# Gate and up weights of a gated MLP beside attention: three buffers and two pairs ahead instead of two buffers and one pair ahead

## The chip, the cores and the metric

One core of one Trainium2 chip. The time of a run is device microseconds from start to end of one launch. All runs quoted here are fast: none lies over 1.5% above the fastest run of its kernel. A profile is one traced execution; its span, first to last instruction, is some 1.8 us shorter than the time of the same run (468.2 against 470.01). Each run also lists the mean clock granted to TensorE, 1.0 being full speed.

## The reference

A transformer block over 2048 tokens of width 448, in bf16: a layernorm, then attention (16 heads of 28, full softmax) and a gated MLP (1792 wide) side by side, all summed.

```
xn = layernorm(x)
q, k, v = split(xn @ wqkv)
o = softmax(q @ k.T * scale) @ v
h = gelu(xn @ w_gate) * (xn @ w_up)
return x + o @ wo + h @ w_down
```

## The kernel before

The kernel runs attention and MLP interleaved. ScalarE takes the exponentials of the scores, 442 tiles of 128x1024; VectorE approximates 70 more. TensorE multiplies the scores into three PSUM buffers, from which ScalarE or VectorE takes them, and fills the time between with everything else: projections, value products, gate, up and down matmuls. A small scheduler in the kernel's own source decides at build time in which order each engine's stream stands. At run time the streams are fixed, and semaphores alone hold them back.

The gate and up matmuls work in pairs of 128 columns. A pair's weights are one tile of 224 KB. There are 28 gate pairs and 28 up pairs: four blocks of 512 tokens, seven pairs each, and the weights are read again for each block.

```python
wgupool = ctx.enter_context(tc.tile_pool(name="wgu", bufs=2))
spool = ctx.enter_context(tc.tile_pool(name="spsum", bufs=3, space=bass.MemoryType.PSUM))
...
def load_w(nm, n):
    if n < NQ * NFC // 2 and (nm, n) not in mlp_w:
        pr = n % (NFC // 2)
        mlp_w[(nm, n)] = w = wgupool.tile([DCH, NDC, 2 * P], BF16, tag=nm, name=nm)
        nc.sync.dma_start(w[:], (wg_v if nm == "wg" else wu_v)[:, :, pr * 2 * P : (pr + 1) * 2 * P])
...
def g_up(Q, pr):
    ht = ht_tiles[(Q, pr)]
    n = Q * NPR + pr
    load_w("wu", n + 1)
    w = mlp_w.pop(("wu", n))
    ...
    for k in range(2):
        ps = aux_tile([P, QT], F32, "up")
        for c in range(NDC):
            yield mm(ps[:], w[:, c, k * P : (k + 1) * P], xnc(Q, c), c == 0, c == NDC - 1, T_MM)
        yield ("ev", T_MM, C_EVAC, lambda k=k, ps=ps: f(k, ps), [("ht", Q, pr, k)])
```

(`g_gate` is the same with "wg". Cuts are marked by "...".) All loads stand in SyncE's queue, in order, together with the small copies that spread the softmax reciprocals. Twice in the kernel ScalarE does 14 GELUs in one batch, at 134 and at 352 us. TensorE uses that time for a run of up pairs, back to back.

The softmax here doesn't subtract the row's maximum and nothing guards it: scores larger than these inputs give would overflow.

Of the kernel before, what the change touches and what calls it, by code (L numbers as in the profile page):

```python
# [38 lines left out]
def kernel(  # L39
# [20 lines left out]
    TPQ = QT // P  # L60
    SCALE = float(Dh) ** -0.5
    NU = NQ * NHG * NKC * 4
    NB = 19
    NVA = 6
    NE = 12
    HALF_MM = 112
# [18 lines left out]
    drpool = ctx.enter_context(tc.tile_pool(name="dr", bufs=3, space=bass.MemoryType.DRAM))  # L85
    onpool = ctx.enter_context(tc.tile_pool(name="on", bufs=6))
    respool = ctx.enter_context(tc.tile_pool(name="res", bufs=2))
    wgupool = ctx.enter_context(tc.tile_pool(name="wgu", bufs=2))
    spool = ctx.enter_context(tc.tile_pool(name="spsum", bufs=3, space=bass.MemoryType.PSUM))
    aux = ctx.enter_context(tc.tile_pool(name="aux", bufs=1, space=bass.MemoryType.PSUM))  # L90

# [18 lines left out]
    wv_ap = A_wqkv.rearrange("(c p) f -> p c f", p=DCH)  # L110
    wst0_t = bpool.tile([P, 2, QT], BF16, tag=f"b{NB - 1}", name="wst0")
    wst0 = wst0_t[0:DCH].rearrange("p a b -> p (a b)")[:, 0 : NDC * 8 * Dh].rearrange(
# [45 lines left out]
# [5 lines that stand above are left out]
# [12 lines left out]
    def xnc(T, c):  # L175
        return xnT0[c // 2][:, c % 2, :] if T == 0 else xnT[T][:, c, :]
# [8 lines left out]
    for lo, hi in LNB:  # L185
        n = hi - lo
# [90 lines left out]
    def aux_tile(shape, dt, name):  # L277
        return aux.tile(shape, dt, tag=bank[0], name=name)

    def mm(ps, lhsT, rhs, start, stop, cost):  # L280
        def emit(lo, hi, cols):
            sl = slice(None) if start else slice(lo, hi)
            for m in range(0, P, P // cols):
                nc.tensor.matmul(  # L284
                    ps[m : m + P // cols, sl],
                    lhsT=lhsT[:, m : m + P // cols],
                    rhs=rhs[:, sl],
                    start=start,
                    stop=stop,
                    skip_group_check=True,  # L290
                    **({"tile_position": (0, m)} if cols > 1 else {}),
                )

        return ("mm", cost, emit, 1 if start else rhs.shape[-1])
# [57 lines left out]

    b_free = list(range(NB))
    b_used = {}
    n_otsb = [0]

    def big(kind, key, shape, dt, name):
        n = b_free.pop(0)
        b_used.setdefault((kind, key), []).append(n)
        return bpool.tile(shape, dt, tag=f"b{n}", name=name)  # L360

    def g_gate(Q, pr):
        ht = ht_tiles[(Q, pr)] = big("h", Q, [P, 2, QT], BF16, "ht")
        n = Q * NPR + pr
        load_w("wg", n + 1)
        w = mlp_w.pop(("wg", n))

        def f(k, ps):
            nc.vector.tensor_copy(ht[:, k, :], ps[:])  # L369
            mlp_done[0] += 1  # L370

        for k in range(2):
            ps = aux_tile([P, QT], F32, "gate")
            for c in range(NDC):
                yield mm(ps[:], w[:, c, k * P : (k + 1) * P], xnc(Q, c), c == 0, c == NDC - 1, T_MM)
            yield ("ev", T_MM, C_EVAC, lambda k=k, ps=ps: f(k, ps), [("g", Q, pr, k)])

    def g_up(Q, pr):
        ht = ht_tiles[(Q, pr)]
        n = Q * NPR + pr  # L380
        load_w("wu", n + 1)
        w = mlp_w.pop(("wu", n))

        def f(k, ps):
            nc.vector.tensor_mul(ht[:, k, :], ps[:], ht[:, k, :])  # L385
            mlp_done[0] += 1
# [6 lines that stand above are left out]
# [292 lines left out]
    for n, batch in enumerate(BATCHES):  # L685
        for Q in batch:
            mlp_items(Q, g_gate, GATE_AT, lambda pr: xkeys(Q), room)
        for Q in batch:
            mlp_items(Q, g_up, UP_AT, lambda pr: [("gelu", Q, pr)], None)
            out_items(Q)  # L690
# [36 lines left out]
    nc.scalar.preload_act_table(AF.Sqrt)  # L727
    xf = bpool.tile([P, 2, QT], BF16, tag=f"b{NB - 2}", name="xf")[:].rearrange("p a b -> p (a b)").bitcast(F32)[:, 0:D]
    mv1 = L["mv"][:, 1, :]
# [583 lines left out]
```

## Time and profile before

| | before |
|---|---|
| time, median of the 3 runs before the prediction | 469.35 us (469.03 to 470.36) |
| span of the profiled run | 468.2 us |
| busy: TensorE, ScalarE, VectorE | 95%, 95%, 77% |
| TensorE idle for late weights | 8.4 us (up), 2.2 us (gate) |
| ScalarE idle for scores | 7.8 us, 1.4 of it before the kernel has got going |

In the views below, a timeline line has the start and the length in us, the engine, the source line, the operation with its tiles, the number of instructions merged into it, and in brackets the idle time before it with what ended it. A line of the list of waits has the total in us, the number of waits and the longest. A line of the groups has the busy time and the mean duration in ns, then the idle time before.

### The profile page before, as it was taken

The page shows a single profiled execution, that of the slowest core. Times are in us where ns is not written, and L with a number is a line of the kernel's source. Part 1 is how long each engine was busy: PE and PEld are TensorE (multiplying, and loading weights), DVE is VectorE, ACT ScalarE, POOL GpSimd, SP SyncE. Part 2 cuts the span into 40 slices and gives each one's busy share as a digit, 9 for nine tenths or more (in the row PEclk, how much of TensorE's full clock was granted, in tenths as well). Part 3 has the DMA queues.
Part 4 walks back from the last instruction along what each step waited for, and adds up shares of the span by engine and source line. Part 5 has one row for each costly group of instructions (what it writes and reads, how often), then busy time and mean ns, then how long its engine had stood idle before and what let it go on. Part 6 is the DMA issues. An engine that isn't in the chain of part 4 may idle for free.

```text
span 468.2 us, 11309 instructions
## 1 busy us (share of the span) xinstructions
PE 444.5 (95%) x4659; PEld 163.8 (35%) x4659; DVE 360.6 (77%) x572; ACT 445.2 (95%) x486; POOL 20.0 (4%) x78
## 2 busy tenths in 40 slices
PE   8899999999987999999999999999997899999994
PEld 4333434333233333333333233333333333333431
DVE  5787686889786877899999897879997677855243
ACT  4899999999999899999999999999999899999992
POOL 5512020000000000000000000000000000000000
PEclk9999999999999999999999999999999999999996
DMA  6920112002133101021202101011203200021001
GB/s 172 298 42 1 41 41 59 2 23 61 34 86 90 30 12 24 12 72 41 72 21 72 41 2 34 21 34 53 60 6 88 81 13 23 22 72 41 14 2 40
DMA packets 43220, 22.81 MB, mean 49 GB/s; under 512 B 8480, under 2 KB 43168, under 8 KB 43168
## 3 DMA queue, kind: packets, MB, share of 16 engines
q1 hardware_dynamic: 42272, 21.65, 17.1%
q8 instruction: 36, 0.59, 0.6%
q10 hardware_dynamic: 896, 0.44, 0.3%
q14 instruction: 16, 0.13, 0.1%
HBM read 20.06 MB, written 1.90 MB: 47 GB/s over the span
## 4 chain that ended last, share of the span: by engine, by line
PE 78%; DMA 9%; DVE 6%; ACT 3%; issue 2%; SPq 0%; POOL 0%; ACTq 0%; DVEq 0%; POOLq 0%
PE st L539 22%; PE ot L587 19%; PE op L284 10%; PE gate L284 10%; PE up L284 8%; PE pp L284 5%; DMA wu<-in_B_w_up_dram 4%; ACT e L551 3%; PE pv L284 3%; DMA x<-in_A_x_dram 2%; DVE w L561 2%; DMA wg<-in_B_w_gate_dram 2%; DVE t L579 2%; DVE ht L369 1%; DVE w L579 0%
## 5 line engine op out<-in xcount | busy, mean ns | idle before, releaser
L551 ACT ACTIVATE e<-st 128x1024 bf16<-128x1024 f32 x442 | 406.7, 1191 | 8.1 <-PE st L539 7.8
L539 PE MATMUL st<-qT,kT 28*128 28x512 bf16 x1024 | 134.3, 382 | 2.3 <-ACT e L551 1.5
L561 DVE TENSOR_SCALAR w<-st 128x1024 f16<-128x1024 f32 x70 | 85.4, 1220 | 22.0 <-PE st L539 22.0
L539 PEld LDWEIGHTS <-kT 28*128 28x128 bf16 x1024 | 42.9, 90 | 124.5 <-issue 120.8
L587 PE MATMUL ot<-e,va 128*32 128x512 bf16 x884 | 80.2, 384 | 0.7 <-ACT e L551 0.5
L579 DVE TENSOR_SCALAR t<-w 128x2048 uint16<-128x2048 f16 x105 | 68.7, 680 | 0.3
L284 PE MATMUL up<-xnT,wu 112*32 112x512 bf16 (+2 forms) x631 | 56.8, 380 | 8.9 <-DMA wu<-in_B_w_up_dram 8.4
L284 PE MATMUL gate<-xnT,wg 112*32 112x512 bf16 (+2 forms) x386 | 62.4, 377 | 2.5 <-DMA wg<-in_B_w_gate_dram 2.2
L284 PE MATMUL op<-wd_sb,ht 128*32 128x448 bf16 (+3 forms) x526 | 56.0, 340 | 0.0
L385 DVE TENSOR_TENSOR ht<-up,ht 128x512 bf16<-128x512 f32 x56 | 38.6, 689 | 20.9 <-PE up L284 15.8
L587 PEld LDWEIGHTS <-va 128*32 128x32 bf16 x1444 | 32.9, 95 | 54.8 <-issue 41.4
L369 DVE CAST ht<-gate 128x512 bf16<-128x512 f32 x56 | 38.3, 686 | 5.9 <-PE gate L284 5.6
L587 PE MATMUL ot<-t,va 128*32 128x512 bf16 x420 | 36.4, 382 | 0.9 <-DVE t L579 0.9
L284 PEld LDWEIGHTS <-wu 112*32 112x32 bf16 (+1 forms) x631 | 21.3, 96 | 36.6 <-DMA wu<-in_B_w_up_dram 14.6
L609 DVE TENSOR_TENSOR otsb<-ot,otsb 128x512 f32<-128x512 f32 x36 | 24.7, 687 | 8.2 <-PE ot L587 7.7
L284 PEld LDWEIGHTS <-wg 112*32 112x32 bf16 (+1 forms) x386 | 19.5, 96 | 27.5 <-issue 10.7
L284 PEld LDWEIGHTS <-ht 128*32 128x32 bf16 (+1 forms) x526 | 22.2, 97 | 19.5 <-issue 6.1
L1113 ACT ACTIVATE ht<-ht 128x1024 bf16<-128x1024 bf16 x28 | 26.7, 1041 | 0.0
L579 DVE TENSOR_SCALAR w<-w 128x2048 uint16<-128x2048 f16 x35 | 24.2, 691 | 0.9
L284 PE MATMUL op<-wo_sb,on 128*32 128x448 bf16 (+2 forms) x170 | 17.8, 345 | 0.0
L284 PE MATMUL pp<-xnT,wq_sb 112*32 112x512 bf16 (+2 forms) x105 | 17.8, 369 | 0.0
L284 PE MATMUL pv<-wv,xnT 112*128 112x448 bf16 (+2 forms) x92 | 15.7, 353 | 1.2 <-DVE kT L329 1.2
(95 smaller groups left out, 220.7 us busy)
## 6 DMA issues: line engine op xcount, KB each, us to landing
wg<-in_B_w_gate_dram SPq DMA_DIRECT2D x28, 224.0 KB
wu<-in_B_w_up_dram SPq DMA_DIRECT2D x28, 224.0 KB
bc<-rr SPq DMA_DIRECT2D x60, 32.0 KB
out_dram<-res SPq DMA_DIRECT2D x15, 112.0 KB
wd_sb<-in_B_w_down_dram SPq DMA_DIRECT2D x1, 1568.0 KB
x<-in_A_x_dram SPq DMA_DIRECT2D x3, 448.0 KB
den<-otsb SPq DMA_DIRECT2D x60, 2.0 KB
wst<-in_A_wqkv_dram SPq DMA_DIRECT2D x2, 392.0 KB
```

The costliest lines, as they stand in the source:

```text
L284: nc.tensor.matmul(ps[m : m + P // cols, sl], lhsT=lhsT[:, m : m + P // cols], rhs=rhs[:, sl], start=start, stop=stop, skip_group_check=Tr ...
L369: nc.vector.tensor_copy(ht[:, k, :], ps[:])
L385: nc.vector.tensor_mul(ht[:, k, :], ps[:], ht[:, k, :])
L539: nc.tensor.matmul(st[:, j * QT : (j + 1) * QT], lhsT=kT[(hg, kc // 4)][32 * hh : 32 * hh + Dh, (kc % 4) * P : (kc % 4 + 1) * P], rhs=qT[( ...
L551: nc.scalar.activation(e[:], s_tiles.pop(k)[:], AF.Exp, scale=SCALE)
L561: nc.vector.tensor_scalar(out=w_tiles[g][1][:, 2 * i * QT : 2 * (i + 1) * QT], in0=s_tiles.pop(k)[:], scalar1=128.0 * SCALE * LOG2E, scala ...
L579: nc.vector.tensor_scalar(out=bits, in0=w[:], scalar1=c, scalar2=None, op0=ALU.add)
L587: nc.tensor.matmul(ot[32 * hh : 32 * hh + 32, :], lhsT=va, rhs=rhs, start=(b, hh) not in started, stop=last, tile_position=(0, 32 * hh), s ...
L609: nc.vector.tensor_add(otsb[:], ot[:], otsb[:])
L1113: nc.scalar.activation(ht[:], ht[:], AF.Gelu_apprx_tanh)
```

## The change

The intent is to have a pair's weights on chip before TensorE comes to it. To make room for the third buffers, the pool of big buffers gives one up.

```diff
-    NB = 19
+    NB = 18
...
-    wgupool = ctx.enter_context(tc.tile_pool(name="wgu", bufs=2))
+    wgupool = ctx.enter_context(tc.tile_pool(name="wgu", bufs=3))
...
         load_w("wg", n + 1)
+        load_w("wg", n + 2)
...
         load_w("wu", n + 1)
+        load_w("wu", n + 2)
```

## The prediction

> **What bounds the kernel now.** I read the page first: busy shares, then the groups with their idle columns.
>
> ```profile
> PE 444.5 (95%) x4659; PEld 163.8 (35%) x4659; DVE 360.6 (77%) x572; ACT 445.2 (95%) x486; POOL 20.0 (4%) x78
> ...
> L551 ACT ACTIVATE e<-st 128x1024 bf16<-128x1024 f32 x442 | 406.7, 1191 | 8.1 <-PE st L539 7.8
> L539 PE MATMUL st<-qT,kT 28*128 28x512 bf16 x1024 | 134.3, 382 | 2.3 <-ACT e L551 1.5
> ```
>
> TensorE and ScalarE are both at 95%, so the share alone does not say which one sets the time. The idle columns do. Once the first exponentials run, ScalarE waits for nothing but scores: 7.8 us in 8 waits. TensorE's matmul ends are modelled, so I do not take its 95% for a full engine. Second view: the list of waits.
>
> ```profile
> SPq L162 <- PE gate L284: 76.7, 13, 17.1
> SPq L162 <- PE up L284: 33.6, 17, 4.1
> ...
> PE up L284 <- DMA wu<-in_B_w_up_dram: 8.4, 9, 1.9
> ACT e L551 <- PE st L539: 7.8, 8, 1.7
> ...
> PE gate L284 <- DMA wg<-in_B_w_gate_dram: 2.2, 2, 1.1
> ```
>
> (The first two lines are from the queue's own list.) The weight queue waits for TensorE to finish with a buffer, and then TensorE waits for the load: 8.4 + 2.2 = 10.6 us. Third view: ScalarE's timeline, which shows where it stood still.
>
> ```profile
> 128.21 4.69 ACT L551 ACTIVATE e<-st 128x1024 bf16<-128x1024 f32 x5 [0.86 <-PE st L539]
> 134.21 13.36 ACT L1113 ACTIVATE ht<-ht 128x1024 bf16<-128x1024 bf16 x14
> 148.89 2.86 ACT L551 ACTIVATE e<-st 128x1024 bf16<-128x1024 f32 x3
> 153.47 60.84 ACT L551 ACTIVATE e<-st 128x1024 bf16<-128x1024 f32 x66 [1.73 <-PE st L539]
> 214.78 47.84 ACT L551 ACTIVATE e<-st 128x1024 bf16<-128x1024 f32 x52 [0.47 <-PE st L539]
> 263.61 87.48 ACT L551 ACTIVATE e<-st 128x1024 bf16<-128x1024 f32 x95 [0.99 <-PE st L539]
> 371.39 53.35 ACT L551 ACTIVATE e<-st 128x1024 bf16<-128x1024 f32 x58 [1.46 <-PE st L539]
> 425.66 33.27 ACT L551 ACTIVATE e<-st 128x1024 bf16<-128x1024 f32 x36 [0.92 <-PE st L539]
> ```
>
> ScalarE runs without a visible pause for 110 us from 17.25, then 61, 48, 87, 53 and 33 us, broken six times. It is the engine that sets the pace; scores are handed to it through three PSUM buffers. Fourth view: TensorE's timeline just before each break. At five of the six the last thing it did was to stand before a weight matmul (1.11 us at 127.14, 0.53 at 213.50, 1.04 at 262.33, 0.81 at 367.95, 1.01 at 424.41), and the sixth, at 153, ends this run:
>
> ```profile
> 138.31 1.91 PE L284 MATMUL up<-xnT,wu 112*32 112x512 bf16 x32 [0.72 <-DMA wu<-in_B_w_up_dram]
> 140.67 1.91 PE L284 MATMUL up<-xnT,wu 112*32 112x512 bf16 x32 [0.45 <-DMA wu<-in_B_w_up_dram]
> 144.52 3.82 PE L284 MATMUL up<-xnT,wu 112*32 112x512 bf16 x64 [1.94 <-DMA wu<-in_B_w_up_dram]
> 149.18 3.82 PE L284 MATMUL up<-xnT,wu 112*32 112x512 bf16 x64 [0.84 <-DMA wu<-in_B_w_up_dram]
> 152.94 0.40 PE L539 MATMUL st<-qT,kT 28*128 28x512 bf16 x4
> ```
>
> A pair of up-projections takes 1.91 us, its 224 KB load some 2.7 us from issue to first use (149.18 less the issue at 146.47), and with two buffers the load can only start when the pair before has ended. So pairs that run back to back wait. The same run at 353 to 371 has waits of 1.26, 0.87 and 0.81.
>
> **What the Trainium skill says.** "DMA: Bandwidth & Descriptors", Anatomy of one DMA, gives (for loads issued by GpSimd) a cost of about 2.0 us plus bytes over 436 GB/s: 229,376 bytes come to 0.53 us, 2.5 us in all. The trace's 2.7 agrees roughly, and says that most of it is latency, so that two loads in flight should overlap well. The rules for kernel authors there advise to issue early and wait late. "Perfetto Trace Analysis", Optimization Strategy, has one find the gaps on the engine that matters and what ends them; by that the worth of the change is ScalarE's 6.4 us, not TensorE's 10.6. The same page, TensorE's lifecycle, says matmul ends are estimated; the trace agrees in that ScalarE never pauses for long stretches while TensorE shows no idle time either.
>
> **The change, part by part.** I compared the built instruction orders of the two kernels, with tile numbers taken off. On TensorE, VectorE, ScalarE and GpSimd they are the same. On the queue four rows differ, and they amount to this: one gate load and one up load are issued additionally at the first pair, and then each later slot carries the load of the pair after the one that it carried before; the last slots are dropped. Loads, bytes and matmuls stay the same in number.
> 1. *NB from 19 to 18.* It only makes room. The built order is unchanged with that edit alone, and a big buffer that is given back goes to the end of the list of free ones, so that I expect no new wait on one: 0 us.
> 2. *Third buffer.* The slot at pair n waited for pair n-1's matmuls (buffer of n-1, for load n+1). It still waits for n-1, but brings load n+2. So the queue keeps its times and every load arrives one pair sooner: what pair m finds is the landing that pair m-1 found before. Check at the single waits, with 2.8 us for a load: gate pair 13's load goes out at 114.14 instead of 124.36, wanted at 126.0; gate 20 at 252.53 instead of 259.00, wanted at 261.3; up 11 at 204.22, wanted at 213.0; up 26 at 417.64, lands about 420.4, wanted at 423.4. All four vanish.
> 3. *Run at 353.* Loads 14 and 15 are already there when it starts; load n+2 goes out at the start of pair n and has 2 x 1.91 = 3.8 us for its 2.7. No wait is left; TensorE ends the run 1.26 + 0.87 + 0.81 = 2.9 us earlier.
> 4. *Run at 134.* Here load 1 still goes out in the slot of pair 0, at 135.49, so the 0.72 us before pair 1 stays. Load 2 follows at once, some 0.5 us of queue time that pushes the broadcast copies behind it. Load 4 goes out at 140.75 as load 3 did, after these broadcasts, and landed then only at 144.5; pair 4 will want it at 138.31 + 3 x 1.91 = 144.0, so 0.5 us stays. Of 3.95 us (0.72 + 0.45 + 1.94 + 0.84) some 2.7 go.
> 5. *What ScalarE gets.* Its first three scores after the table load last until 148.89 + 2.86 = 151.75. The next are multiplied at 152.94 now and at about 150.2 after; with half a microsecond for the product they are there a microsecond before they are wanted. At 369.93 the same: 370.86 becomes 367.9. So both breaks close wholly.
> Sum on ScalarE's path: 0.86 + 1.73 + 0.47 + 0.99 + 1.46 + 0.92 = 6.43 us. Nothing is added to that path. What lies before the first exponentials and after the last one (458.9 to the end, 9.3 us) has no weight load in it and stays. 469.35 - 6.43 = 462.9 us, or 1.4% less.
>
> **Rivals.**
> *(a) VectorE takes the wait over.* Idle time of VectorE from the trace's records: 0.8 us in 195 to 215, 0.9 in 215 to 240, 1.6 in 240 to 264. It is 96% busy where two of the breaks lie (0.47 and 0.99), and much of its idle time there is the same stall. If VectorE cannot follow, those two come back as waits for freed PSUM or for its terms: up to 1.4 us lost, 464.4. Against: it still has about 1.8 us to spare there, and the largest breaks lie where it has 5 to 7 us.
> *(b) TensorE becomes the bound.* If its stream is really full, the removed stalls give its whole 10.6 us less what stays, some 9 us and 460.2, since then ScalarE would be following it. Against: ScalarE's unbroken stretches, which need TensorE to be held back by the three score buffers and not the other way.
> *(c) The load only moves.* Two loads and the broadcasts in flight together stretch each other, or the queue's added slot delays the normalisation; then the runs keep half their waits. As both runs have 1 to 1.5 us to spare, ScalarE would see little of it: 463.5 to 465. If the queue were held up as before with no load earlier, 469. Against: the transfers of queue 1 fill 17% of the engines' time over the span.
> *(d) Deeper prefetch is hidden anyway.* It would be if ScalarE had stock at the breaks. It has not: a break of TensorE of 1.04 us at 262 makes one of 0.99 at ScalarE.
>
> **Range and chances.** I put about two thirds on the sum holding within 0.8 us, most of the rest on (a) and (c), which take up to half of it, and little on (b). That shifts the middle by half a microsecond: 463.4 us, 8 in 10 between 461.9 and 466.2. Faster by over 2% needs 459.96, 9.4 us less, which only (b) brings: 0.03. Slower by over 2% would need new stalls of over 9 us, in an unchanged order: 0.01. Within 2%: 0.96.
>
> **What would show it.** Right: TensorE's waits for both weights fall from 10.6 to some 1.2 us, all in the run at 134 (before pairs 1 and 4); ScalarE's wait for scores falls from 7.8 to about 1.4, its start; busy times stay. Its exponentials run in one stretch from the first table switch back (near 148) to the second switch. Step 4 is wrong if pairs 2, 3 or 5 wait; (a) is right if ScalarE has gaps in 195 to 264 with TensorE waiting for VectorE before them. The prediction is wrong if weights no longer wait and the time stays above 466.2: then a stall that I took for the cause was hidden by another that ends just after.

## The result

The changed kernel takes 461.25 us (median of 4 runs, 460.88 to 461.91) against 469.19 (4 runs, 468.68 to 470.36). The ratio is 0.9829, with a 95% interval of 0.9807 to 0.985. Ratios here are the mean time of one kernel's fast runs over that of the other's of the same rounds, so they are not quite the ratio of the medians. The prediction was 463.4 us in a range of 461.9 to 466.2. The time lies below that range: the gain is 7.9 us, where its sum came to 6.43 and its middle to 6.

The page of the changed kernel, busy shares and groups (two source lines were added, so L551 is now L553 and L539 is L541):

```profile
PE 443.3 (96%) x4659; PEld 166.0 (36%) x4659; DVE 359.7 (78%) x572; ACT 444.5 (97%) x486; POOL 20.0 (4%) x78
...
L553 ACT ACTIVATE e<-st 128x1024 bf16<-128x1024 f32 x442 | 406.0, 1197 | 1.9 <-PE st L541 1.6
L541 PE MATMUL st<-qT,kT 28*128 28x512 bf16 x1024 | 135.7, 382 | 2.9 <-ACT e L553 2.0
```

The work is the same in number and nearly so in time. ScalarE's idle time before exponentials has gone from 8.1 to 1.9 us. The list of waits, the queue's own first:

```profile
SPq L162 <- PE gate L284: 73.8, 12, 16.8
SPq L162 <- PE up L284: 29.6, 16, 3.9
...
PE st L541 <- ACT e L553: 2.0, 7, 0.5
...
PE up L284 <- DMA wu<-in_B_w_up_dram: 1.7, 2, 1.1
ACT e L553 <- PE st L541: 1.6, 2, 0.9
```

The queue still waits for TensorE as long as it did (76.7 and 33.6 before), but TensorE hardly waits for the queue: its idle time for weights is 1.7 us instead of 10.6, and no gate wait is left. ScalarE's timeline has become short:

```profile
16.73 114.69 ACT L553 ACTIVATE e<-st 128x1024 bf16<-128x1024 f32 x125 [0.94 <-PE st L541]
...
147.40 198.74 ACT L553 ACTIVATE e<-st 128x1024 bf16<-128x1024 f32 x216
...
362.12 89.19 ACT L553 ACTIVATE e<-st 128x1024 bf16<-128x1024 f32 x97
454.49 0.97 ACT L1283 CAST res<-fa 128x448 bf16<-128x448 f32 x2 [3.18 <-PE fa L1274]
```

All six pauses are gone: one stretch to the first GELU batch, one of 199 us between the batches, one to the end. TensorE's timeline in the two runs of up pairs:

```profile
137.77 5.82 PE L284 MATMUL up<-xnT,wu 112*32 112x512 bf16 x96 [1.14 <-DMA wu<-in_B_w_up_dram]
144.12 5.73 PE L284 MATMUL up<-xnT,wu 112*32 112x512 bf16 x96 [0.53 <-DMA wu<-in_B_w_up_dram]
149.78 0.40 PE L541 MATMUL st<-qT,kT 28*128 28x512 bf16 x4
...
350.67 12.40 PE L284 MATMUL up<-xnT,wu 112*32 112x512 bf16 x204
```

In the first run TensorE waits for weights before pair 1 and before pair 4 and nowhere else; in the second it does not wait at all.

So the mechanism came out as forecast, and the question is the size: where do the other 1.5 us come from? The two traces give a first part. Before, the first long stretch of exponentials begins here:

```profile
17.25 110.11 ACT L551 ACTIVATE e<-st 128x1024 bf16<-128x1024 f32 x120 [0.72 <-PE st L539]
```

From the start of the first long stretch to the end of the last exponential it is 458.93 - 17.25 = 441.68 us before (425.66 + 33.27 is the end) and 451.31 - 16.73 = 434.58 after (362.12 + 89.19). That is 7.10 us less, not 6.43. Look at one pause before, in ScalarE's timeline in a narrow window:

```profile
125.20 2.16 ACT L551 ACTIVATE e<-st 128x1024 bf16<-128x1024 f32 x2
128.21 1.94 ACT L551 ACTIVATE e<-st 128x1024 bf16<-128x1024 f32 x2 [0.86 <-PE st L539]
```

Undisturbed, these exponentials start 0.90 us apart, yet the record of the second one lasts 1.25 us (0.91 + 1.25 = 2.16): a record reaches into the time of the next. The second one here starts at 126.11, and without a pause the next would have started at 127.01. It started at 128.21. Counted by starts, 1.20 us is lost, and the profile shows 0.86 as idle. Below, each pause is counted in this way from the single records, against the same pair of exponentials in the changed kernel, and once more by the ends of the two records instead of their starts:

| pause at | shown as idle, us | start to start before | after | loss by starts | loss by ends |
|---|---|---|---|---|---|
| 128.2 | 0.86 | 2.11 | 0.90 | 1.21 | 0.96 |
| 153.5 | 1.73 | 2.76 | 1.09 | 1.67 | 1.67 |
| 214.8 | 0.47 | 1.67 | 0.97 | 0.70 | 0.58 |
| 263.6 | 0.99 | 2.19 | 0.97 | 1.22 | 1.10 |
| 371.4 | 1.46 | 2.49 | 0.90 | 1.59 | 1.57 |
| 425.7 | 0.92 | 2.18 | 0.99 | 1.19 | 1.03 |
| sum | 6.43 | | | 7.57 | 6.90 |

Of the 7.57, 0.47 is taken back in between, which leaves 7.10. The records say why. In an undisturbed stretch the starts are 0.904 us apart but the ends 0.917, so that as a rule each record is some 13 ns longer than the one before it: 1.02 us after the start at 17.25, and up to 1.42 later. A pause sets the length back to about 1.03. Counting starts therefore counts as lost a lead that the starts had gained. By ends the sum, 6.90, is closer to the 7.10: in five of the six it is the idle time shown and 0.10 or 0.11 more, since the first exponential after a pause ends 1.03 us after its start and the others end 0.917 us apart. The 7.10 is that of one pair of traces: over all profiles without a half clock in the middle the same stretch takes 440.7 to 442.2 us in the kernel before (three profiles) and 434.2 to 434.6 in the changed one (four profiles; these counts take in the experiments below that only keep the end busy). The other 0.8 of the 7.9 us cannot be read from these two traces; start and end of the kernel differ by 0.5 and 1.1 us between them, which may be chance.

### The profile page after: what moved, and what is told of

Same layout as the page of the kernel before. It is cut to its first block, busy times and chain, and to the rows that moved or that the text cites. A ratio compares the mean times of both kernels' runs of the same rounds, so it can differ in the third digit from the quotient of the medians.

```text
span 459.5 us, 11311 instructions
## 1 busy us (share of the span) xinstructions
PE 443.3 (96%) x4659; PEld 166.0 (36%) x4659; DVE 359.7 (78%) x572; ACT 444.5 (97%) x486; POOL 20.0 (4%) x78
## 4 chain that ended last, share of the span: by engine, by line
PE 78%; DVE 6%; ACT 6%; DMA 4%; SPq 3%; issue 2%; ACTq 0%; POOL 0%; DVEq 0%; POOLq 0%
PE st L541 22%; PE ot L589 18%; PE op L284 11%; PE gate L284 10%; PE up L284 8%; PE pp L284 5%; ACT e L553 3%; PE pv L284 3%; DVE w L563 2%; ACT ht L1115 2%; DMA x<-in_A_x_dram 2%; DVE t L581 1%; SPq L415 1%; DVE ht L370 1%; DMA wu<-in_B_w_up_dram 1%
## 5 line engine op out<-in xcount | busy, mean ns | idle before, releaser
L553 ACT ACTIVATE e<-st 128x1024 bf16<-128x1024 f32 x442 | 406.0, 1197 | 1.9 <-PE st L541 1.6
L541 PE MATMUL st<-qT,kT 28*128 28x512 bf16 x1024 | 135.7, 382 | 2.9 <-ACT e L553 2.0
L541 PEld LDWEIGHTS <-kT 28*128 28x128 bf16 x1024 | 43.6, 90 | 125.5 <-issue 121.5
L284 PEld LDWEIGHTS <-wu 112*32 112x32 bf16 (+1 forms) x631 | 22.8, 96 | 28.1 <-issue 8.8
```

Source lines behind the costliest of these rows:

```text
L284: nc.tensor.matmul(ps[m : m + P // cols, sl], lhsT=lhsT[:, m : m + P // cols], rhs=rhs[:, sl], start=start, stop=stop, skip_group_check=Tr ...
L541: nc.tensor.matmul(st[:, j * QT : (j + 1) * QT], lhsT=kT[(hg, kc // 4)][32 * hh : 32 * hh + Dh, (kc % 4) * P : (kc % 4 + 1) * P], rhs=qT[( ...
L553: nc.scalar.activation(e[:], s_tiles.pop(k)[:], AF.Exp, scale=SCALE)
```

## The experiments

Fifteen kernels ran, in four sets. Kernels of a set ran on the same chip and share their runs of the kernel before. All gave correct results.

### First set: scatter, and the parts of the change

**The two kernels again, unedited.**

> The kernel before, unedited, as a measure of scatter and of the clock at the end of each run. The gain on record is 7.9 us where the six pauses of ScalarE that the profile shows sum to 6.43 us. Theory A (the pauses cost more than is shown, since the record of an exponential runs about 0.25 us into the next one's time; start to start the stretch of exponentials shrank by 7.1 us): the rest, 0.8 us, is scatter of start and end, and the runs of this kernel lie within 468.5 to 470.5 with no steady end at half clock. Theory B (the change also shortens the end, since this kernel always finishes at half the matmul clock and the changed one does not): every run here shows a granted clock of about 0.992 and the end is always about 1 us longer.

> The changed kernel, unedited. Theory A: 7.1 us less than before, give or take 0.5, so 462.0; clock at the end as mixed as before's. Theory B: again 7.9 us less, about 461.2, with clock near 1.0 in most runs.

Measured: before 468.61 us (6 runs, 466.87 to 469.43), and its 11 shared runs 469.0 (466.95 to 472.98); after 460.89 (6 runs, 460.32 to 461.85), ratio 0.9812 (0.9774 to 0.985). The gain is 7.7 to 8.1, so it is no accident of the first four runs. Theory A, that all beyond 7.1 is scatter, is in doubt. Theory B, an end always at half clock, is too: one run of the unedited kernel had the clock at 1.0 and took 467.29, and a changed one ended at half clock with an end of 9.2 us. What stands out is another thing. The kernel before scatters over 6 us and has runs at 472 to 473; the changed one scatters over 1.5.

**18 big buffers alone.**

```diff
-    NB = 19
+    NB = 18
```

> Only the count of big buffers goes from 19 to 18. Prediction and both theories: 0 us, within 0.5 of before. If the layout of the on-chip memory has a part in the gain, up to 0.8 us less.

Measured: 469.63 us (468.3 to 470.26), ratio 0.9988 (0.9946 to 1.0031). The room that the change takes costs nothing, and gains nothing. But its profile has a surprise. The pause of ScalarE after the first run of up pairs, 1.73 us in the profile of before (and 1.9 to 2.8 in the later profiles without a half clock there), is 3.45 us here, and the matmul clock is recorded at half from 144.5 to 147.9 us, just after TensorE's longest wait for weights. That became a third theory.

**Three buffers, loads at their old place in the queue.**

```diff
-    NB = 19
+    NB = 18
-    wgupool = ctx.enter_context(tc.tile_pool(name="wgu", bufs=2))
+    wgupool = ctx.enter_context(tc.tile_pool(name="wgu", bufs=3))
```

> Three buffers (and 18 big ones), but each load still stands at its old place in the queue, one pair ahead. If the buffer is what held the loads up (theory 1), the two back-to-back runs and all single breaks vanish where the queue had nothing else ahead of the load: some 5 to 7 us less. If the place in the queue counts too (theory 2), the breaks where the load stood behind other transfers stay, above all the gate load at 124 which went out only after four broadcasts: some 1 to 2 us less gain than the whole change. If the distance alone counts (theory 3), hardly any gain.

Measured: 464.06 us (462.66 to 465.94), ratio 0.9882 (0.984 to 0.9924): some 5 of the 8 us. A third buffer lets a load at its old place go out earlier, because what it waits for, the matmuls on the buffer it overwrites, lies one pair further back. Where something else stands ahead of the load in the queue, it does not help. ScalarE's timeline of this kernel, then the queue's:

```profile
129.80 4.69 ACT L551 ACTIVATE e<-st 128x1024 bf16<-128x1024 f32 x5 [0.78 <-PE st L539]
...
154.29 195.98 ACT L551 ACTIVATE e<-st 128x1024 bf16<-128x1024 f32 x213 [0.95 <-PE st L539]
```

```profile
124.00 1.93 SPq L413 DMA_DIRECT2D bc<-rr  x4
126.03 0.37 SPq L162 DMA_DIRECT2D wg<-in_B_w_gate_dram  x1
```

The gate load still goes out only after four broadcasts, and its pause stays, as theory 2 said. So does one after the first run of up pairs. The four others are gone. Buffers and place both count, the buffers for more. (Three of the six runs, at a clock of 0.999, took 462.7 to 463.4. This profiled run, at 465.94 the slowest of its six, also had a half clock at 18 to 21 us that cost two pauses of 0.6 us near the start.)

### Second set: the weights apart, and the clock

**Up weights alone, gate weights alone.** Each has a pool of its own, three buffers and two pairs ahead for one of them:

```diff
-    NB = 19
+    NB = 18
     wgupool = ctx.enter_context(tc.tile_pool(name="wgu", bufs=2))
+    wuupool = ctx.enter_context(tc.tile_pool(name="wuu", bufs=3))
... (load_w takes an up tile from wuupool)
         load_w("wu", n + 1)
+        load_w("wu", n + 2)
```

> Three buffers and two pairs ahead for the up weights alone. By the pauses shown, 1.73 + 0.47 + 1.46 + 0.92 = 4.6 us less than before; counted start to start 4.9; with the half clock in the runs gone as well, 5.5 to 6. The pauses at 128 and 263 stay.

> The same for the gate weights alone. By the pauses shown 0.86 + 0.99 = 1.85 us less; counted start to start 2.2. No part of the clock: these two waits of one microsecond lie amid busy matmuls. The runs over 470 stay possible.

Measured: up alone 463.46 us (463.03 to 463.66), ratio 0.9886, 5.2 us under the 468.7 of before in these rounds; gate alone 467.34 (466.4 to 469.65), ratio 0.9972, 1.4 us under, with an interval that reaches to 0.9999. The gain of the up weights lies between the 4.9 and the 5.5 that I had written, the gate's is nearer to the pauses shown than to the start-to-start count and too scattered to tell them apart. Together they make 6.6 us, where the whole change brought 7.7 to 8.1 on another chip and, with one load more at the start (below), 7.4 in this set; whether that is scatter was not tested. The pauses that stay with the up weights alone are the two of the gate, as expected:

```profile
127.71 4.69 ACT L553 ACTIVATE e<-st 128x1024 bf16<-128x1024 f32 x5 [0.90 <-PE st L541]
...
260.14 87.48 ACT L553 ACTIVATE e<-st 128x1024 bf16<-128x1024 f32 x95 [0.72 <-PE st L541]
```

**Idle matmuls in the waits of the kernel before.** `junk(bank, k)`, a helper of the kernel, issues k matmuls with weights of zero. They go into the bank that the pair is about to start, so they change no result:

```diff
             ps = aux_tile([P, QT], F32, "up")
+            if k == 0:
+                junk(ps[:], {3: 6, 5: 2, 16: 4, 18: 2, 20: 2}.get(n, 0))
```

> The kernel before, with 16 idle matmuls of about 0.2 us put in the two runs of up pairs where TensorE stands and waits for weights (6, 2, 4, 2, 2 of them, before pairs 3, 5, 16, 18, 20); they write into the bank that the pair is about to start afresh. The waits stay, TensorE merely looks busy in them. Clock theory (part of the gain over the 6.43 us comes from the matmul clock, which the record of the run with 18 buffers shows at half from 144.5 to 147.9, after the longest wait, and which lengthened its pause at 154 from 1.7 to 3.4 us): no half clock within 130 to 375, no run over 470, the median perhaps 0.5 under before. Rival (the half clock there is chance and costs nothing on average): the same scatter as before, 467 to 473.

Measured: 468.14 us (466.68 to 469.01), ratio 0.9987 (0.9965 to 1.0008). No run over 470, against 2 of the 11 of before beside it, and no half clock within the profile's runs of up pairs. That is what the clock theory wants, but six runs cannot show it.

**Second up load at the start, in the changed kernel.**

```diff
         load_w("wu", 0)
+        load_w("wu", 1)
```

> The changed kernel with the second up load issued at the start already, so that the last of TensorE's weight waits (0.7 us before pair 1 of the first run, of 1.7 left) goes. If ScalarE sets the time, 0 us against the changed kernel (460.5 to 461.5, some 8 less than before); if TensorE does, 0.7 us less.

Measured: 461.32 us (460.52 to 462.56), ratio 0.9844: no gain, as expected if ScalarE sets the time. But the test was less clean than planned. TensorE's weight wait did not shrink; it moved to pair 4 and was 1.8 us in one piece, and the clock fell to half after it, from 145.5 to 148.9, with a pause of 1.69 us at ScalarE. So in this one profile waits that were merely moved together brought the half clock into the changed kernel.

### Third set: what a stall costs, the end, and the queue

**A stall put back.** Ten idle matmuls before each of the four single pairs, in the changed kernel:

```diff
             ps = aux_tile([P, QT], F32, "gate")
+            if k == 0:
+                junk(ps[:], {13: 10, 20: 10}.get(n, 0))
...
             ps = aux_tile([P, QT], F32, "up")
+            if k == 0:
+                junk(ps[:], {11: 10, 26: 10}.get(n, 0))
```

> The changed kernel with ten idle matmuls of 0.216 us, 2.16 us, put in front of four pairs where the kernel before stood waiting (gate 13 and 20, up 11 and 26). It asks what a stall of TensorE costs. If ScalarE has no stock there (pauses counted start to start are the loss): each costs 2.2 us less what stock there is, at most 0.1 to 0.9, so 5 to 8.6 us in all, and the pauses that the profile shows are smaller than the loss by about 0.25 us each, since an exponential's record reaches that far into the next one's time. If the pause shown were the loss, the sums would agree. If ScalarE had stock, under 2 us.

Measured: 468.98 us (468.67 to 469.55), 8.1 us over the 460.85 of the changed kernel with filled end from the same set. Forty idle matmuls of 0.216 us are 8.64. TensorE's stalls pass to ScalarE nearly whole, so there is no stock of scores at these places. The pauses that the profile shows:

```profile
128.40 4.69 ACT L557 ACTIVATE e<-st 128x1024 bf16<-128x1024 f32 x5 [1.73 <-PE st L545]
...
214.37 47.84 ACT L557 ACTIVATE e<-st 128x1024 bf16<-128x1024 f32 x52 [1.93 <-PE st L545]
264.15 87.48 ACT L557 ACTIVATE e<-st 128x1024 bf16<-128x1024 f32 x95 [1.93 <-PE st L545]
...
425.53 33.27 ACT L557 ACTIVATE e<-st 128x1024 bf16<-128x1024 f32 x36 [1.89 <-PE st L545]
```

They sum to 7.48; the stretch of exponentials grew by 7.65 (442.23 against 434.58). My "0.25 us each" is right at the pause itself (start to start, the stall at 128 costs 2.08 us and shows 1.73), but part of it comes back before the next. By ends the four pauses cost 7.91 us. In sum the idle time shown was 0.2 us under the loss here and 0.7 under it in the kernel before. Note also the scatter: 0.9 us over six runs. Full stalls of busy idle matmuls do not bring the slow runs back. What this run can't say is which engine sets the time: were TensorE the bound, the 8.64 us would show as well.

**The end kept busy**, in the changed kernel and in the one before (three, two and one idle matmuls):

```diff
     preload(0)
+    junk(fa[:, QT:], 3)
...
         do_pv(clock["PE"], "q")
+    junk(fa[:, QT:], 2)
... (after the four matmuls with selc)
+    junk(fa[:, QT:], 1)
```

> The changed kernel with six idle matmuls in the end, where TensorE waits for VectorE and for the last exponentials, to keep the matmul clock up. The end (last exponential to last instruction) took 8.16 us where the clock stayed full until then and 9.22 where it fell to half at 1.8 us after the last exponential. Clock theory: the end takes 8.1 to 8.4 in the profile and the clock of most runs is 0.998 to 1.0; 0 to 0.5 us less than the changed kernel in the median. Rival (the idle matmuls delay the end): up to 0.5 us more.

> The same six idle matmuls in the end of the kernel before. If part of the gain on record comes from an end at half clock that this kernel mostly has and the changed one mostly has not (14 of its first 17 runs at 0.985 to 0.994, 3 of 10 of the changed one's), this gains more here than there: 0.5 to 0.9 us less than before, and its difference to the changed kernel with the same edit is 7.1 to 7.4. If not, the same small change for both, and their difference stays near 8.

Measured: changed kernel 460.85 us (460.4 to 461.68), before 469.76 (468.03 to 470.59; ratio 0.9994 to the unedited one). The edit does what it should: the end takes 8.3 to 8.4 us in both profiles. It gains nothing in the median of either. (In the fourth set the kernel before with a busy end is at a ratio of 0.9973 to the unedited one, with an interval of 0.9942 to 1.0005, so a small gain is not excluded.) What decides on theory B is the difference between the two kernels: by the means it is 8.6 and 8.1 us with busy ends (third and fourth set) and 8.0 and 8.7 without (result and first set). So theory B falls: the end at half clock is not where the missing gain lies. With the end kept busy ("quiet end" below) the clock of a run tells of what happened earlier: the profiles still fall to half clock in the last 1.5 to 2.8 us, and one window of 3.41 us at half clock takes a further 0.0036 off the mean over 468 us. The six runs of before fall into two groups: 468.03 and 468.54 at 0.997, and 469.73, 469.79, 470.10 and 470.59 at 0.993 or 0.994. Where the half clock lay can be seen only in the profiled run (470.10), which is of the slower group. Its stretches around the first run of up pairs (columns: stretch, length, busy time of PE, PEld, DVE, ACT, POOL, then clock, DMA share, GB/s) and TensorE's timeline there:

```profile
141.30:144.70 3.40, 1.10 (x24) 0.32 (x12) 1.44 (x3) 3.40 (x5) 0.00 (x0) 1.00 0.49 140
144.70:148.20 3.50, 3.34 (x32) 1.28 (x36) 0.69 (x1) 3.48 (x4) 0.00 (x0) 0.51 0.00 1
```

```profile
144.86 5.37 PE L284 MATMUL up<-xnT,wu 112*32 112x512 bf16 x64 [2.45 <-DMA wu<-in_B_w_up_dram]
```

In the first stretch TensorE stands for most of 3.4 us; in the next its clock is 0.51, and two pairs take 5.37 us instead of 3.82. ScalarE's pause after it is 4.04 us.

**Broadcasts from another queue**, in the changed kernel:

```diff
-            nc.sync.dma_start(bc[32 * j : 32 * j + 32, :], rr[j : j + 1, :].to_broadcast([32, QT]))
+            nc.gpsimd.dma_start(bc[32 * j : 32 * j + 32, :], rr[j : j + 1, :].to_broadcast([32, QT]))
```

> The changed kernel with the broadcasts of the reciprocals issued by GpSimd, so that no weight load stands behind them in the queue. Step 4 of the prediction said that the fourth load of the first run is late for that reason (0.53 us waited there). Right: that wait goes and 0.7 to 1.1 us before pair 1 stays; time 0 against the changed kernel, since ScalarE has a microsecond in hand there. Wrong if the wait stays, or if the time falls by over 0.5 us.

Measured: 460.88 us (460.33 to 462.01), the same as the changed kernel. Both waits did the opposite of what I wrote. The one before pair 1 went, since its load now left at 132.22, a microsecond before the run. The one before pair 4 stayed, and after the run TensorE had to wait for ScalarE:

```profile
142.69 5.83 PE L284 MATMUL up<-xnT,wu 112*32 112x512 bf16 x96 [0.68 <-DMA wu<-in_B_w_up_dram]
...
149.27 0.39 PE L541 MATMUL st<-qT,kT 28*128 28x512 bf16 x2 [0.43 <-ACT e L553]
```

Its load left at 138.07 by the queue's record and was waited for until 142.69, 4.6 us, with no broadcast ahead of it in its queue; the broadcasts were issued from GpSimd at 137.82 to 139.78. So in this profile the order in the queue was not what made the load late. But the wait before pair 4 is not a fixed one: of the four profiles of the changed kernel (after, after again, and the two with a busy end) only the first has it. In the three others the same load, behind the same broadcasts, was there within 3.5 us. Whether the transfers stretch each other or the load's time just scatters stays open. TensorE waited for weights for 0.68 us here, 1.0 less than in the first profile but only 0.2 less than in the others, and the time did not notice: as a test of what bounds the kernel this is a weak one. The second line shown says more: TensorE stood 0.43 us until ScalarE freed a score buffer.

### Fourth set: the half clock

> The kernel before with idle matmuls in its end, run again beside the next. Its first six runs lay in two groups: 468.0 and 468.5 at a clock of 0.997, and 469.7 to 470.6 at 0.993 or 0.994; the profile of one of the second group shows the clock at half from 144.7 to 148.2, after a stretch of 3.4 us in which TensorE was busy for 1.1. Clock theory: again two groups, some 1.8 us apart, and the clock tells them apart.

> The same with idle matmuls also in the waits of the two up runs (8, 3, 5, 3, 3). The waits for weights stay as long. Clock theory: one group, at 468.0 to 468.6, all at a clock of 0.997 or more, 7.1 to 7.5 us over the changed kernel with the same end. Rival (the two groups have another cause): two groups again, or all near 470.

> The changed kernel with idle matmuls in its end, for the difference: one group at 460.4 to 461.7. Counted start to start ScalarE's stretch is 7.1 us shorter than before's without the half clock, so 7.1 to 7.5 less than the filled kernel and 8 to 9 less than the median of the unfilled one.

The filled kernel has the edit of the end and this one:

```diff
             ps = aux_tile([P, QT], F32, "up")
+            if k == 0:
+                junk(ps[:], {3: 8, 5: 3, 16: 5, 18: 3, 20: 3}.get(n, 0))
```

Measured: before with quiet end 468.67 us (467.75 to 470.91), again in two groups that the clock tells apart. Taking its twelve runs of both sets together, six have a clock of 0.997 or more and average 468.35 us, six have 0.993 or 0.994 and average 470.16: 1.8 us apart, with no overlap. The changed kernel with the same end: 460.89 (460.67 to 461.16), and 460.89 as the mean of its ten runs of both sets. The profile of before with quiet end is this time of the faster group. It is a close partner of the one shown above: at the same place the wait is about as long (2.37 against 2.45 us), but no half clock follows, and ScalarE's pause is 2.31 us instead of 4.04, which is 1.7 less:

```profile
144.36 3.82 PE L284 MATMUL up<-xnT,wu 112*32 112x512 bf16 x64 [2.37 <-DMA wu<-in_B_w_up_dram]
```

The filled kernel: 469.06 us (468.42 to 470.24), and all six runs at 0.997 to 1.0. The group with the low clock is gone, as the clock theory said, with the waits for weights still there. But the time is not at the 468.0 to 468.6 that it wanted: the mean of the six is 469.18, against 469.05 for the unfilled kernel beside it. Perhaps the idle matmuls overshot: in this profile the pause at ScalarE after the second run of up pairs is 2.11 us, against 1.23 in the profile of the unfilled kernel of this set. That is not shown either, since the profiled run is the fastest of the six (468.42), and its whole stretch of exponentials is not longer (441.91 us against 442.18). So it is supported, by none of six runs against six of twelve, that the low clock comes with these waits; that removing it alone saves time is not shown.

No experiment beat the changed kernel by more than the scatter.

## Why the prediction was wrong

**What bounds the kernel (right).** ScalarE set the pace. In the changed kernel it runs three unbroken stretches, and within them nine in ten exponentials end 0.916 to 0.918 us after the one before; TensorE in turn waits for ScalarE to free score buffers (2.0 us in 7 waits). Stalls of TensorE come through almost whole (8.1 us for 8.64), because ScalarE has no stock of scores.

**Steps 1 and 2 (right).** 18 buffers: ratio 0.9988. The queue's waits are what they were (73.8 and 29.6 us against 76.7 and 33.6), and all four single waits vanished.

**Step 3 (right).** No wait in the second run of up pairs.

**Step 4 (right in size, in part wrong in reason).** In the first profile waits of 1.14 and 0.53 us remain before pairs 1 and 4, where 0.72 and 0.5 were forecast; in the three other profiles of the changed kernel one of 0.84 to 0.90, before pair 1 alone. Counted from the start of the GELU batch, which itself comes 1.5 us earlier in the changed kernel, the first scores after the run are multiplied at 17.06 us in the first profile and at 16.1 to 16.5 in the others; the forecast was 16.0 (150.2 less 134.21), and before it was 18.73. So in the first profile the microsecond in hand of step 5 was used up, and ScalarE lost 0.19 us there (1.09 instead of 0.90 between two starts). That the fourth load is late because it stands behind broadcasts did not hold in the one profile of the run that moved them. The 2.5 us for a load was an estimate from the figures that the Trainium skill's "DMA: Bandwidth & Descriptors", Anatomy of one DMA, gives for loads issued by GpSimd, which these are not; "two loads in flight should overlap well" did not hold in every trace, since this load took 4.1 and 4.6 us in two of them.

**Step 5 and the sum (the step that failed).** "0.86 + 1.73 + 0.47 + 0.99 + 1.46 + 0.92 = 6.43 us" takes the idle time shown between two records for the time lost. All six breaks closed as it said, but they were mis-sized: they cost 6.90 us by ends (7.57 by starts), and in the same pair of traces the whole stretch of exponentials shrank by 7.10. And a term was missing: in about half the runs of the kernel before, as far as their clock tells, the waits come with a second cost. The longest of them can leave most of one stretch of 3.4 us without matmuls; the clock is then at half for the next 3.4 us. With the end kept quiet the runs at the low clock are 1.8 us slower, and with 6 of 12 runs in that group this is 0.9 us on average. The changed kernel with the same end has none such among ten runs. The budget by these runs, all with quiet ends: 470.16 or 468.35 before, 460.89 after; 7.5 us without the half clock, which the 7.1 of the stretch covers to within the scatter, and 0.9 of the clock: 8.4, against 7.9 in the result. The first part is shown. The second rests on the two groups of runs and on one pair of profiles (4.04 against 2.31 us); the filled kernel lost the low clock and did not get faster, so its size stays open.

**The rivals.** (a) did not come: VectorE is idle for only 0.6 to 0.7 us in each of the stretches 195 to 215, 215 to 240 and 240 to 264 of the changed kernel, but ScalarE has no pause there. (Before, VectorE was 96% busy around the break of 0.47 but 93% around that of 0.99: 22.4 of 24 us.) (c) came in small part: the first run kept 1.67 of its 3.95 us in the first profile, at a cost to ScalarE of 0.19, and 0.84 to 0.90 in the others. Because I gave these two a third of the weight and saw nothing on the other side but a TensorE-bound kernel, I moved the middle half a microsecond up, away from the result. (b) named a time (460.2) near the measured one, but for a reason that the experiments deny. That the gain would stay under 2% was right.

**What the traces of one run could not tell.** The profile of before that I read had no half clock in the middle. Its runs, 469.03 to 470.36, hid that: the slower group was there to see only in the later runs, with the end kept busy.

## What to carry to other kernels

Size a pause of ScalarE from the end of one record to the end of the next, or better by the whole stretch, and not by the idle time between records: here the idle time came to 6.43 us, the starts to 7.57, the ends to 6.90 and the stretch to 7.10. When a load is late, ask for both its buffer and its place in the queue: a third buffer alone brought 5 of 8 us here, and the earlier place the rest. Look twice at waits of TensorE that come close together: after stretches of 3.4 us in which it was busy for 31 to 47% its clock was at half for the next 3.4 us, in some runs and not in others, so look at the scatter and the clock of many runs before sizing a gain. Compare times of two traces from an event that both have (here the start of the GELU batch), since the faster kernel is ahead by then.

## What the Trainium skill lacked or had wrong

- "TensorE: Matmul & The Clock Gate", What's actually happening, has the free-running window of 3.4 us, and the runs agree: a half clock before the end of the kernel lasted 3.41 us in all four profiles that have one, and by the mean clock came in 6 of 12 runs of one kernel. Its table of the two states has the clock fall after an idle window. Here it fell after windows, counted from the rise of the clock, in which TensorE was busy by the trace for 31% (before with quiet end), 38% (18 buffers alone), 43% (three buffers alone, near its start) and 47% (second up load at the start). It stayed up after windows of 50% (three buffers alone) and 54 to 57%, the emptiest in the middle of five other profiles (changed kernel, up alone, gate alone, before again, before with quiet end again). So in mid-kernel half a window is nearer to the limit than an idle one. At the end of the kernel it also fell after windows of 65%, so the busy share is not what is counted, or not alone.
- "Perfetto Trace Analysis", Optimization Strategy, has one look at the gaps between slices on the engine that matters. I found no page that draws from its account of the records that a gap understates the loss: 0.86 us shown for 0.96 lost by ends, 6.43 for 7.10 over the kernel.
- "ScalarE: Activation LUTs", What ACT_TABLE_LOAD costs, gives an overlap of about 93 ns between back-to-back ACTIVATEs. In this kernel, with 128x1024 from PSUM, records averaging 1.19 us start some 0.91 us apart, an overlap of about 0.28, and the records grow from 1.02 to 1.42 us along a stretch. The GELUs, 128x1024 from SBUF, agree with the page: 1.041 us long, 0.948 apart.
- No page that I found says how much a 224 KB load stretches when small broadcasts run beside it: 2.7 us from issue to first use alone; for the load of pair 4, with broadcasts of 32 KB and another load in flight, 4.1 and 4.6 in two profiles and 3.5 at most in three others.
